# Two bias loads moved behind the DMA transposes, and a table of scheduler rules for 128 stretches of 16 score tiles

## The chip, the cores and the metric

The kernel runs on one core of a Trainium2 chip. The metric is device time in microseconds (us) of one execution; lower is better. Five engines are named as in the profile: PE (matrix), DVE (vector), ACT (activation functions), POOL and SP. SP issues every DMA of this kernel, all on one queue and in the order in which the program was built.

## The reference, cut to what matters

```python
xn = layernorm(x)                                  # x: 2048 x 640
qkv = (xn @ wqkv).reshape(S, 3, 32 heads, 20)      # attention with 32 heads of width 20
p = softmax(q @ k.T * 20 ** -0.5)                  # per head 2048 x 2048
s = (p @ v) @ wo                                   # per head, then 640 x 640
h = layernorm(xn)                                  # token MLP: it mixes the 2048 rows
u = gelu(h.T @ w1 + b1)                            # 640 x 1536
g = silu((u @ w2 + b2).T)                          # 2048 x 640
out = x + s * g
```

b1 (1536 values) and b2 (2048 values) are the two biases of the token MLP.

## The kernel before, in words

**Tiling.** The attention is cut into 8 head groups of 4 heads and 4 query blocks of 512, hence 32 passes; one pass has 16 key chunks of 128, each with 4 heads: 64 score tiles of 128 x 512, and 2048 tiles in all. Each tile is made by one matmul of 32 rows (`emit_st`, L1160), and up to four tiles of different heads can share the PE. A tile goes one of two ways. The ACT way: two or three tiles lie in neighbouring PSUM banks (`ACT_GROUPS`, L255: banks 0 to 2, and 3 and 4) and one ACT instruction takes the exponential of all of them into `pt_sb` (`emit_exp`, L1189). The DVE way: a whole key chunk (4 tiles, one per head) is turned into an approximate exponential by integer arithmetic on bfloat16 bit patterns: one DVE instruction per tile (L1200) and three shifted copies per chunk (L1224) that are averaged through pre-scaled copies of v (`vs_sb`). Chunks 2, 5, 8, 11 and 14 of a pass may go to the DVE (`RC`, L259). The products with v gather in bank 6 (L1240). At the end of a pass the DVE transposes and normalises the sum (`ep_steps`, L1334 to L1355).

**Stages.** First x and the weights are loaded. The layer norm of the 16 row blocks runs on DVE, with the power on POOL (`ln_steps`, L478 to L496). Blocks 0 to 3 are transposed on PE; blocks 4 to 15 by 12 DMA transposes (`xTd_steps`, L533), each of which waits for the L496 instruction of its block. Then the q and k projections of head group 0 (L573) and the v projections (L681). The other projections, the token MLP (L588, with evictions on L758 and the activation chain on L773 to L789) and the output projection (L872) are placed between the score tiles of later passes. The q and k of the other head groups travel through DRAM (L614, L653). Two small DMAs bring b1 and b2 into `bload_sb` (L444, L446; 2 bytes per element and partition), and two DVE instructions halve them (L1385, L1387).

**What sets the order.** Nothing is ordered on the chip. A planner in Python (`schedule`, from L403) keeps a model time for every engine and picks, in a loop (L1806), the next step of the engine that can start first; `pe_cands` (L1560) and `eng_cands` (L1781) list the candidates with a priority each. What it picks is appended to that engine's list, and every engine then executes its list strictly in order, with a semaphore wait wherever another engine's result is needed. Class constants steer the picks: `SLACK` and `MINJ` (how near to ACT's next need PE may start other work), `ROOM` (free slots of `pt_sb`), `LEND` (an ACT bank lent to a DVE tile), `LATE`, `PARTS`, `CONFL`, `FGAP` and others. The function `behind` (L1076) compares the projection and MLP work done with a straight line over the score tiles; when it is more than 3000 behind, the DVE may claim no new chunk (L1082) and may not use bank 7. DMAs are modelled by one bytes-per-time cost (`dma`, L166 and L412).

The lines that set a DMA's place and the DVE's share:

```python
def d_claimable():                                   # L1081
    if behind() > self.BEH_D:
        return None
...
add_job("bias", [ ...b1h on bl1..., ...b2h on bl2... ], ("xn15",), 43.0)   # L1384
```

Of the kernel before, what the change touches and what calls it, by code (L numbers as in the profile page):

```python
# [6 lines left out]
dt = mybir.dt  # L7
# [32 lines left out]
class Prog:  # L40
# [40 lines left out]
    def _add(self, eng, ceng, fn, reads, writes, name, extra_req=(), cost=100.0, tail=None):  # L81
# [51 lines left out]
        if ceng not in self.COMPUTE:  # L133
            start = max(start, 700.0)
            self.T[eng] = start + 450.0
            self.pipe = max(self.pipe, start + 600.0) + cost
            t.fin = self.pipe + (1200.0 if self.pipe < 2500.0 else 2800.0 if cost > 800.0 else 1400.0)
        else:
            self.T[eng] = start + cost
            self.busy[eng] += cost  # L140
            t.fin = start + cost + (self.TAIL[eng] if tail is None else tail)
# [23 lines left out]

    def dma(self, fn, reads=(), writes=(), name="dma", lane=None, cost=3000.0, over=()):  # L166
        if lane is None:
            lane = self.lane_rr
            self.lane_rr = (self.lane_rr + 1) % self.n_lanes
        ceng = f"d{lane}"  # L170
        prev = self.ctasks[ceng][-1] if self.ctasks[ceng] else None
        extra = [prev] if prev is not None else []
        for s in over:
            if s.w is not None:
                extra.append(s.w)
            extra.extend(s.readers.values())
        t = self._add("sp", ceng, fn, reads, writes, name, extra_req=extra, cost=cost)
        t.need_inc = True
        return t
# [67 lines left out]
class _Kern:  # L247
# [34 lines left out]
    QC = ((0.5, 3.0), (3.2, 6.4), (9.0, 13.5), (14.0, 18.0), (19.0, 22.0))  # L282
    LINE = (2.0, 31.7)
    BEH_D, BEH_J = 3000.0, 3000.0
    PARTS = (2,)
    DX = (1, 2, 3)
    XDC = 300000
    V1A, V1B = 0.8, 4.0
# [15 lines left out]
    def build(self):  # L304
# [4 lines left out]
        with es:  # L309
# [45 lines left out]
            pr.emit(sems)  # L355

    def schedule(self):
        pr, t, nc = self.prog, self.t, self.nc
# [53 lines left out]
        def dma(fn, reads, writes, name, nbytes, over=()):  # L412
            pr.dma(fn, reads=reads, writes=writes, name=name, cost=nbytes / 355.0, over=over)

# [24 lines left out]
        def small(fn):  # L439
# [3 lines left out]
            return f  # L443
        dma(small(lambda e: e.dma_start(bload_sb[:, 0:FC], B_b1.rearrange("(fc p) -> p fc", p=P))), [], [S_("bl1")],  # L444
            "dma_b1", 3000)
        dma(small(lambda e: e.dma_start(bload_sb[:, FC:FC + NB], B_b2.rearrange("(b p) -> p b", p=P))), [],  # L446
            [S_("bl2")], "dma_b2", 4000)

        pr.dve(lambda e: e.memset(on_sb[:], 0.0), writes=[S_("on")], name="on0", cost=200)
# [80 lines left out]
        def xTd_steps(b):  # L530
            dst = xnT_sb[:, :, b * 128:(b + 1) * 128]
            src = regC[:, b, :]
            return [("dma", lambda e: e.dma_start_transpose(dst, src), [S_(f"h{b}")], [S_(f"xTb{b}")], f"xTd{b}", self.XDC),  # L533
                    ("tag", f"xTd{b}")]
# [305 lines left out]
        def reload_steps():  # L840
            steps = []
            for c in range(4):
                for tb in range(NTB):
                    ws = S_(f"oTa_{c}_{tb}")
                    oT_slots.setdefault(("oTa", c), []).append(ws)
                    d = oT_sb[:, c, tb * 512:(tb + 1) * 512]
                    src = ok_dram[tb * 512:(tb + 1) * 512, c * 128:c * 128 + 128]
                    steps.append(("dma", lambda e, d=d, src=src: e.dma_start_transpose(d, src),
                                  [S_(f"okd{pass_of[(G, tb)]}_{g}") for G in range(L6) for g in range(GH)] + [S_("okz")], [ws],
                                  f"oTt{c}_{tb}", 131072, xall))  # L850
            return steps + [("tag", "oT")]
# [214 lines left out]
        def a_left(q):  # L1066
            n = sum(4 for c in range(NB) if (q, c) not in claimed)
            if a_cur[1] is not None and a_cur[0] == q:
                n += GH - a_cur[2]
            return n  # L1070

        jw = [0.0]
        JTOT = (self.NB * 5 * mm(480) + 36 * 5 * mm(512) + FC * NB * (mm(512) + mm(128)) * 2.0
                + 12 * 5 * (mm(512) + mm(128)))

        def behind():  # L1076
            x0, x1 = self.LINE
            x = nclaim[0] / UP
            return JTOT * min((x - x0) / (x1 - x0), 1.0) - jw[0]

        def d_claimable():  # L1081
            if behind() > self.BEH_D:  # L1082
                return None
# [29 lines left out]
        def d_bank():  # L1113
            if not dveready[0]:
                return None
            if dbank[0] == "free" and fin_bank(DB):
                return DB
            if self.SHARE and JB in freebanks and len(dop1) < 2 and not ramp[0] and behind() < self.BEH_J:
                return JB
# [256 lines left out]
        for g in range(GH):  # L1376
# [5 lines left out]
        add_job("qk1pad", pads, tuple(f"qk0_{w}_{tb}" for w in (0, 1) for tb in range(NTB)) + ("qk0_1_0a",), 41.0)  # L1382
        add_job("r2", r2_steps(), sum((xtag(gb) for gb in range(4)), ()), 43.0)
        add_job("bias", [  # L1384
            ("dve", lambda e: e.tensor_scalar(b1h_sb[:, :], bload_sb[:, 0:FC], 0.5, None, ALU.mult), [S_("bl1")],  # L1385
             [S_("b1h")], "b1h", 120.0),
            ("dve", lambda e: e.tensor_scalar(b2h_sb[:, :], bload_sb[:, FC:FC + NB], 0.5, None, ALU.mult), [S_("bl2")],  # L1387
             [S_("b2h")], "b2h", 120.0), ("tag", "bias")], ("xn15",), 43.0)

# [170 lines left out]
        def pe_cands(T):  # L1560
# [3 lines left out]
            if us:  # L1564
# [3 lines left out]
                for gi in range(len(self.ACT_GROUPS)):  # L1568
                    grp = self.ACT_GROUPS[(last_grp[0] + 1 + gi) % len(self.ACT_GROUPS)]
                    if grp_state[grp] == "free" and all(fin_bank(b) and b not in lent for b in grp):  # L1570
# [189 lines left out]
        def do_step(j, eng):  # L1760
            s = j.steps[j.i]
            j.i += 1
            if s[0] == "ev":
                n = s[8]
                fn = ev_fn(s, eng)
                cost = ac(n) if eng == "act" else (dv(n, 0.53) if s[7].startswith("xTe") else dp(n))
                getattr(pr, eng)(fn, reads=s[5], writes=s[6], name=s[7], cost=cost)
            elif s[0] == "pe":
                if j.bank and not ramp[0]:
                    jw[0] += s[5]  # L1770
                if len(s) > 6:
# [5 lines left out]
            else:  # L1777
                getattr(pr, s[0])(s[1], reads=s[2], writes=s[3], name=s[4], cost=s[5])
            settle(j)

        def eng_cands(eng, T):  # L1781
            c = []
            for j in active:
# [3 lines left out]
                elif s[0] == "ev" and (eng == "dve" or (eng == "act" and (ramp[0]))):  # L1787
                    c.append((min(j.prio - 3.0, 24.0) if not ramp[0] else j.prio - 3.0, pr.ready(eng, s[5], s[6]),
                              lambda j=j: do_step(j, eng)))
# [3 lines left out]
            if eng == "dve":  # L1793
# [3 lines left out]
                if dtop and tfree:  # L1797
                    d, k = dtop[0]
                    b0, b = d["tl"][0], tfree[0]
                    c.append((38.0, pr.ready("dve", [S_(f"dt{b0}_{g}") for g in range(4)],  # L1800
                                             [S_(f"dt{b}_{g}") for g in range(4)]), emit_top))
            return c

        bank_off = set()
        guard = 0
        while True:  # L1806
            guard += 1
            assert guard < 400000
            if ramp[0] and "v0_14" in done and "qk0_0_3" in done:
# [77 lines left out]
```

## Time and profile before

Seven runs: median 773.91 us (769.78 to 774.86). The profiled execution took 773.91 us itself, and its span from the first to the last instruction is 772.1 us, so 1.8 us lie around the span. Engine instructions before and after the change, as far as they differ, stand in the section on the change.

| | busy us | share of the span | instructions |
|---|---|---|---|
| PE matmuls | 729.9 | 95% | 10114 |
| DVE | 716.1 | 93% | 1348 |
| ACT | 737.3 | 96% | 709 |
| POOL | 13.2 | 2% | 19 |

How to read it: the busy time of an engine is the union of its records. Records of neighbouring ACT or DVE instructions overlap a little[...], so the mean length of a record times the count is more than the busy time. The chain of work that ended last runs through ACT for 75% of the span and through PE for 20%. The mean granted PE clock is 0.992 of full speed.

### The profile page before, as it was taken

How to read it: one execution, taken by the hardware profiler on the slowest of the kernel's cores; microseconds unless marked ns; L12 is line 12 of the kernel's file. 1: busy time of each engine (PE TensorE's matmuls, PEld its weight loads, DVE VectorE, ACT ScalarE, POOL GpSimd, SP SyncE). 2: the span in 40 equal slices, each digit the busy share in tenths (PEclk: the TensorE clock that was granted, in tenths of full speed). 3: DMA queues.
4: the chain of work that ended last, by engine and by line, in shares of the span. 5: the costliest groups of instructions: out<-in, count | busy, mean ns of one | idle time of the engine just before them, and what ended most of it. 6: DMA issues, size and time to landing. Idle time of an engine off the chain costs nothing.

```text
span 772.1 us, 22825 instructions
## 1 busy us (share of the span) xinstructions
PE 729.9 (95%) x10114; PEld 240.3 (31%) x10128; DVE 716.1 (93%) x1348; ACT 737.3 (96%) x709; POOL 13.2 (2%) x19
## 2 busy tenths in 40 slices
PE   8699999999999999999999999999999999999997
PEld 3232222223332322232322323232333332332222
DVE  7589999999999999898999999999999999999996
ACT  4599999999999999999999999999999999999993
POOL 3200000000000000000000000000000000000000
PEclk9899999999999999999999999999999999999999
DMA  9481111101120121031030014120335420041101
GB/s 265 85 161 43 34 30 33 23 18 27 38 64 13 20 51 45 16 84 20 14 84 12 19 27 93 45 53 6 96 78 69 122 65 18 7 149 46 48 12 69
DMA packets 117143, 42.53 MB, mean 55 GB/s; under 512 B 75300, under 2 KB 115876, under 8 KB 116996
## 3 DMA queue, kind: packets, MB, share of 16 engines
q1 hardware_dynamic: 117044, 41.07, 22.7%
q8 instruction: 79, 1.29, 0.7%
q14 instruction: 20, 0.16, 0.1%
HBM read 26.37 MB, written 10.22 MB: 47 GB/s over the span
## 4 chain that ended last, share of the span: by engine, by line
ACT 75%; PE 20%; DVE 2%; DMA 1%; issue 0%; SPq 0%; POOL 0%; ACTq 0%
ACT pt_sb L1189 73%; PE ps_all L1160 6%; PE ps_all L588 6%; PE ps_all L1240 5%; PE ps_all L872 1%; PE ps_all L573 1%; ACT zt_sb L779 1%; ACT zt_sb L784 1%; DMA wqk_sb<-in_A_wqkv_dram 1%; DMA xnT_sb<-regC 0%; SPq L418 0%; DVE dt_sb L1200 0%; PE ps_all L681 0%; DVE regC L496 0%; DVE dt_sb L1224 0%
## 5 line engine op out<-in xcount | busy, mean ns | idle before, releaser
L1189 ACT ACTIVATE pt_sb<-ps_all 128x1024 bf16<-128x1024 f32 (+1 forms) x671 | 717.1, 1203 | 3.6 <-PE ps_all L1160 2.5
L1200 DVE TENSOR_SCALAR dt_sb<-ps_all 128x512 uint16<-128x512 f32 x488 | 325.4, 680 | 25.9 <-PE ps_all L1160 24.7
L1160 PE MATMUL ps_all<-qk_sb 32*128 32x512 bf16 x2048 | 292.3, 386 | 27.1 <-ACT pt_sb L1189 23.6
L1224 DVE TENSOR_SCALAR dt_sb<-dt_sb 128x2048 uint16<-128x2048 uint16 x366 | 241.1, 684 | 1.7
L1160 PEld LDWEIGHTS ps_all<-qk_sb 32*128 32x128 bf16 x2048 | 74.2, 91 | 289.2 <-ACT pt_sb L1189 203.0
L1240 PE MATMUL ps_all<-pt_sb,v_sb 128*21 128x512 bf16 x1560 | 123.1, 382 | 0.1
L1240 PE MATMUL ps_all<-dt_sb,vs_sb 128*21 128x512 bf16 x1464 | 121.9, 384 | 0.0
L588 PE MATMUL ps_all<-regC,regA 128*32 128x512 bf16 (+1 forms) x1536 | 67.0, 301 | 0.0
L588 PE MATMUL ps_all<-regB,regA 128*32 128x128 bf16 (+1 forms) x1536 | 66.5, 301 | 0.1
L588 PE MATMUL ps_all<-xnT_sb,wqk_sb 128*32 128x512 bf16 x640 | 49.3, 383 | 0.3
L1240 PE MATMUL ps_all<-dt_sb,v_sb 128*21 128x512 bf16 x488 | 48.6, 389 | 0.6 <-DVE tr_sb L1334 0.5
L1240 PEld LDWEIGHTS ps_all<-pt_sb,v_sb 128*21 128x21 bf16 x1560 | 29.7, 91 | 51.1 <-issue 37.4
L1240 PEld LDWEIGHTS ps_all<-dt_sb,vs_sb 128*21 128x21 bf16 x1464 | 28.6, 91 | 32.3 <-issue 23.5
L588 PEld LDWEIGHTS ps_all<-regC,regA 128*32 128x32 bf16 x1536 | 28.8, 96 | 27.3 <-issue 13.1
L588 PEld LDWEIGHTS ps_all<-regB,regA 128*32 128x32 bf16 x1536 | 28.0, 96 | 26.5 <-issue 12.9
L872 PE MATMUL ps_all<-wv_sb,xnT_sb 128*128 128x128 bf16 (+3 forms) x150 | 27.3, 297 | 1.5 <-issue 1.3
L1334 DVE STREAM_TRANSPOSE tr_sb<-ps_all 128x512 f32<-128x512 f32 x32 | 22.6, 707 | 4.3 <-PE ps_all L1240 4.3
L588 PE MATMUL ps_all<-wv_sb,xnT_sb 128*32 128x480 bf16 x320 | 21.3, 369 | 0.0
L588 PEld LDWEIGHTS ps_all<-xnT_sb,wqk_sb 128*32 128x32 bf16 x640 | 14.0, 95 | 20.8 <-issue 10.0
L1240 PEld LDWEIGHTS ps_all<-dt_sb,v_sb 128*21 128x21 bf16 x488 | 12.2, 90 | 26.2 <-issue 21.2
L758 DVE TENSOR_SCALAR zt_sb<-ps_all,b2h_sb 128x512 bf16<-128x512 f32 (+1 forms) x32 | 17.1, 543 | 1.9 <-PE ps_all L588 1.8
L987 DVE CAST v_sb<-ps_all 128x480 bf16<-128x480 f32 (+1 forms) x23 | 13.8, 601 | 4.4 <-PE ps_all L681 3.6
(73 smaller groups left out, 293.3 us busy)
## 6 DMA issues: line engine op xcount, KB each, us to landing
regA<-in_B_w_dram SPq DMA_DIRECT2D x6, 1024.0 KB
regA<-in_B_w_dram SPq DMA_DIRECT2D x8, 768.0 KB
qk_sb<-qk_scratch_dram SPq DMA_DIRECT2D x56, 80.0 KB
qk_scratch_dram<-qs_sb SPq DMA_DIRECT2D x32, 128.0 KB
regA<-in_A_x_dram SPq DMA_DIRECT2D x6, 640.0 KB
ok_scratch_dram<-on_sb SPq DMA_DIRECT2D x96, 20.0 KB
out_dram<-regC SPq DMA_DIRECT2D x3, 640.0 KB
wqk_sb<-in_A_wqkv_dram SPq DMA_DIRECT2D x2, 480.0 KB
```

The source lines that it names most:

```text
L573: steps.append(("pe", lambda e, dc=dc, lhsT=lhsT: e.matmul(ps(bk, n), lhsT, xnT_sb[:, dc, tb * 512 + c0:tb * 512 + c0 + n], start=(dc == 0 ...
L588: fns.append(lambda e, c=c, e_=e_: e.matmul(oc(c, e_), lhsT[:, c:e_], rhs, start=start, stop=stop, tile_position=(0, c)))
L758: steps.append(("dve", lambda e, z=z, i=i, jj=jj: e.tensor_scalar(z[:, c0:c0 + n], ps(bk, n, i * n), 0.5, bias[:, jj:jj + 1], ALU.mult, AL ...
L779: steps.append(("act", lambda e: e.activation(tt_, tt_, AF.Tanh, scale=1.5957691216), [stt], [stt], f"th{j}", ac(640)))
L872: steps.append(("pe", lambda e, c=c, k=k: e.matmul(ap, oT_sb[0:k, c, b * 128:(b + 1) * 128], wo_ap[0:k, c, c0:c0 + n], start=(c == 0), sto ...
L987: return lambda e: e.tensor_copy(dst, src)
L1160: pr.pe(lambda e, outp=outp, lhsT=lhsT, rhs=rhs, g=g: e.matmul(outp, lhsT, rhs, start=True, stop=True, tile_position=(32 * g, 0)), reads=[ ...
L1189: tk = pr.act(lambda e: e.activation(outp, inp, AF.Exp, scale=math.log(2.0) / 128.0), reads=[bank_slot[b] for b in banks[:n]], writes=[S_( ...
L1200: tk = pr.dve(lambda e: e.tensor_scalar(w, src, WOFF, 0.0, ALU.add, ALU.max), reads=[bank_slot[bk]], writes=[S_(f"dt{d['tl'][0]}_{g}")], n ...
L1224: tk = pr.dve(lambda e: e.tensor_scalar(dst, src, dk, None, ALU.add), reads=[S_(f"dt{b0}_{g}") for g in range(4)], writes=[S_(f"dt{b}_{g}" ...
L1240: pr.pe(lambda e: e.matmul(outp, lhsT, rhs, start=(k == 0), stop=last, tile_position=(0, 32 * g)), reads=reads, writes=[bank_slot[AB]], na ...
L1334: steps.append(("dve", lambda e: e.transpose(tr_sb[:, :], ps(AB)), [bank_slot[AB]], [S_("tr")], f"epT{q}", 632.0))
```

## The change

1. The DMAs of b1 and b2 are no longer issued with the input loads. They become a job that starts after the four small copies inside `qk_sb` ("qk1pad"), so behind the 12 DMA transposes on SP's queue. The two DVE instructions that halve the biases move with them.
2. The planner gets a cost of its own for a DMA transpose: 1320 ns on the queue, and 2700 ns until it has landed.
3. `behind` is removed. What steered the DVE's claims and bank 7 by it is gone; in its place stands a flag `DON`.
4. Fourteen rules become settable (`OPTS`). A table `PLAN` has one row of 14 digits per stretch of 16 score tiles; at the start of each stretch `tune` sets the rules from its row.

```diff
-        dma(small(lambda e: e.dma_start(bload_sb[:, 0:FC], B_b1...)), [], [S_("bl1")], "dma_b1", 3000)
-        dma(small(lambda e: e.dma_start(bload_sb[:, FC:FC + NB], B_b2...)), [], [S_("bl2")], "dma_b2", 4000)
...
+        add_job("bload", [("dma", ...dma_b1...), ("dma", ...dma_b2...), ("tag", "bload")], ("qk1pad",), 43.0)
         add_job("bias", [ ...b1h..., ...b2h..., ("tag", "bias")],
-                ("xn15",), 43.0)
+                ("bload",), 43.0)
...
         def d_claimable():
-            if behind() > self.BEH_D:
+            if not self.DON:
                 return None
...
-            if self.SHARE and JB in freebanks and len(dop1) < 2 and not ramp[0] and behind() < self.BEH_J:
+            if self.SHARE and JB in freebanks and len(dop1) < 2 and not ramp[0]:
                 return JB
...
+    OPTS = (
+        ("SLACK", (120.0, 40.0, 200.0, 320.0)), ("MINJ", (640.0, 320.0, 1000.0)), ("ROOM", (3, 6, 0)),
+        ("DRIDE", (400.0, 150.0, 700.0)), ("LEND", (900.0, 300.0, 1500.0, 0.0, 2500.0)),
+        ("PARTS", ((2,), (2, 1), (3, 1), (1,), ())), ("LATE", (2.0, -9.0, 99.0)), ("DON", (True, False)),
+        ("LONE", (False, True)), ("CONFL", (True, False)), ("TOPP", (38.0, 22.0)), ("EVP", (24.0, 36.0)),
+        ("FGAP", (40.0, 150.0)), ("GROT", (1, 0)),
+    )
+    PLAN = ("00010000000000", "00000000000000", "00100000001000", ...)
+    def tune(self, w):
+        if w < len(self.PLAN):
+            for (name, vals), i in zip(self.OPTS, self.PLAN[w]):
+                setattr(self, name, vals[int(i)])
...
         while True:
             guard += 1
+            if nclaim[0] >= win * self.WIN:
+                self.tune(win)
+                win += 1
```

`LEND`'s first value is 900 where the constant was 1100. The functions that the steps call are the same as before; what the change makes of them is another order. What differs in the number of instructions, counted in the two built programs:

| instruction | before | after |
|---|---|---|
| exponential of 2 tiles, ACT (128 x 1024) | 453 | 423 |
| exponential of 3 tiles, ACT (128 x 1536) | 218 | 235 |
| exponential of 1 tile, ACT (128 x 512) | 0 | 1 |
| first DVE step of a tile (128 x 512) | 488 | 496 |
| shifted copy, DVE (128 x 2048) | 366 | 372 |
| matmul with zeros that keeps the PE active (L1255) | 116 | 104 |

All other instructions are the same in number, but for one q eviction in the ramp that the DVE does as a copy of k instead (and ACT the other). In the DVE's list the two halving instructions stood right behind the last layer norm block; now they stand behind the first six L1200 and three L1224 instructions. The order on PE, DVE, ACT and SP differs throughout.

## The prediction, made before the changed kernel was run

> **What bounds the kernel now.** I read the engines' busy row and the chain of waits first, then the costliest groups.
>
> ```profile
> span 772.1 us, 22825 instructions
> PE 729.9 (95%) x10114; PEld 240.3 (31%) x10128; DVE 716.1 (93%) x1348; ACT 737.3 (96%) x709; POOL 13.2 (2%) x19
> ...
> ACT 75%; PE 20%; DVE 2%; DMA 1%; issue 0%; SPq 0%; POOL 0%; ACTq 0%
> ...
> L1200 DVE TENSOR_SCALAR dt_sb<-ps_all 128x512 uint16<-128x512 f32 x488 | 325.4, 680 | 25.9 <-PE ps_all L1160 24.7
> ```
>
> ACT carries the chain. Three engines are over 90% busy, so the next question is where ACT is not. The groups by form and ACT's timeline tell it:
>
> ```profile
> L1189 ACT ACTIVATE pt_sb<-ps_all 128x1024 bf16<-128x1024 f32 x453 | 451.1, 1064 | 1.4 <-PE ps_all L1160 0.7 <-PE ps_all L1240 0.3
> L1189 ACT ACTIVATE pt_sb<-ps_all 128x1536 bf16<-128x1536 f32 x218 | 325.4, 1493 | 2.1 <-PE ps_all L1160 1.7 <-PE ps_all L1240 0.2
> ```
>
> ```profile
> 19.06 2.40 ACT L1189 ACTIVATE pt_sb<-ps_all 128x1024 bf16<-128x1024 f32 x2
> 28.45 0.60 ACT L986 ACTIVATE qk_sb<-ps_all 128x512 bf16<-128x512 f32 x1 [7.00 <-PE ps_all L573]
> 30.59 0.60 ACT L989 ACTIVATE qk_sb<-ps_all 128x512 bf16<-128x512 f32 x1 [1.54 <-PE ps_all L573]
> 31.13 1.02 ACT L1189 ACTIVATE pt_sb<-ps_all 128x1024 bf16<-128x1024 f32 x1
> ```
>
> Between 50 and 750 us ACT is busy 696.8 of 700 us (table of windows). Its one large hole is in the ramp: no exponential runs from 21.46 to 31.13. The chain there leads to a DMA transpose. SP's timeline and PE's:
>
> ```profile
> 8.64 2.67 SPq L423 DMA_DIRECT2D wqk_sb<-in_A_wqkv_dram  x2
> 11.36 2.15 SPq L444 DMA_DIRECT2D bload_sb<-in_B_b_dram  x1
> 13.55 4.17 SPq L446 DMA_DIRECT2D bload_sb<-in_B_b_dram  x1
> 17.76 22.36 SPq L533 DMA_TRANSPOSE xnT_sb<-regC  x12
> ```
>
> ```profile
> 20.44 1.04 PE L1255 MATMUL ps_all<-wp_sb,zw_sb 128*21 128x512 bf16 x16
> 26.50 4.05 PE L573 MATMUL ps_all<-xnT_sb,wp_sb 128*128 128x512 bf16 x9 [5.02 <-DMA xnT_sb<-regC]
> 30.48 1.03 PE L1160 MATMUL ps_all<-qk_sb 32*128 32x512 bf16 x5
> ```
>
> The two bias loads hold SP for 6.3 us right ahead of the transposes, while the first two blocks for these were normalised by 14.32 (L496 on DVE, 13.53 for 0.79 us). PE idles from 21.48 to 26.50, and then the clock is half:
>
> ```profile
> core 0: us, PE busy (x) PEld busy (x) DVE busy (x) ACT busy (x) POOL busy (x), PEclk, DMA share, GB/s
> 14.00:16.00 2.00, 2.00 (x23) 1.07 (x20) 1.16 (x5) 1.89 (x3) 0.69 (x1) 1.00 1.08 342
> 16.00:18.00 2.00, 1.80 (x17) 0.68 (x15) 1.97 (x9) 2.00 (x3) 0.00 (x0) 1.00 1.14 260
> 24.00:26.00 2.00, 0.00 (x0) 0.00 (x0) 2.00 (x6) 0.00 (x0) 0.00 (x0) 0.81 0.50 99
> 26.00:28.00 2.00, 1.50 (x4) 0.74 (x6) 1.32 (x7) 0.00 (x0) 0.00 (x0) 0.50 0.76 152
> ```
>
> **Step 1, the ramp.** Blocks 6 and 7 are normalised at 16.77 and 17.52, so by the L496 rows alone the fourth transpose could be issued at 17.5 to 18.1 and land 2.6 us later (the chain shows 2.59 from the issue at 23.46 to its landing), at 20.7. A rule speaks against so much: the Trainium skill, page "DMA: Bandwidth & Descriptors", section "Queues, rings and completion order", says that a DMA engine takes the descriptors of a queue in ring order. The transposes would then wait for the input loads ahead of them, and these move over 340 GB/s until 16 and end at about 17.2. Four transposes at the 1.23 us that one takes in the trace give 22.1, and with the completion up to 23.4. I take 22.0 for PE's start, nearer the rule, against 26.05 (23.46 + 2.59).
>
> PE then waits from about 21.5 to 22.0, not 5 us. The page "TensorE: Matmul & The Clock Gate", section "Part 1: The HAM clock gate", says that an idle window of about 3.4 us halves the clock; the trace agrees (0.81, then 0.50, after an idle stretch of 5.0 us). With at most 1.9 us idle (23.4 - 21.5) the clock stays, and the ten L573 matmuls take 10 x 0.22 = 2.2 us (five of them, warm, go by from 44.75 to 45.93) where 26.05 to 30.48 was 4.4. So: projections done 24.2, q eviction on ACT 0.6, first exponential 24.8 instead of 31.13: 6.3 us. Part is given back at the next blocks: the DVE evicts k ahead of normalising blocks 8 to 11, and PE may be late for their projection by 0 to 1.5 us; I take 0.7. **Net -5.6 us, between -3.5 and -7.**
>
> **Step 2, ACT's own work.** The tiles by ACT go from 453x2 + 218x3 = 1560 to 423x2 + 235x3 + 1 = 1552, in 659 instructions instead of 671. By the rows a third tile costs 1493 - 1064 = 0.429 us. The rest of an instruction is 1.064 - 0.858 = 0.206, of which 0.135 overlaps its neighbour ((453 x 1.064 + 218 x 1.493 - 717.1)/671), so 0.071. 8 x 0.429 + 12 x 0.071 = **-4.3 us**, all on ACT and so on the path.
>
> **Step 3, the DVE and PE.** Eight more tiles cost the DVE 8 x 0.667 (325.4/488) + 6 x 0.659 (241.1/366) = +9.3 us. They lie beside ACT: in the windows from 50 to 750 the DVE is busy 667.4 of 700, and L1200 waits for PE 24.7 us. If that cover were gone they would cost all 9.3. PE gets less to do: counted in the two orders there are 1206 instead of 1229 changes between score, product and full matmuls, about 0.10 each (a group of three scores starts at 14.14 and the next kind at 14.46; the wave itself takes 0.22), and 31 fewer score waves: 2.3 + 6.8 = 9 us. PE waits for ACT anyway, so I count nothing. The 12 fewer zero matmuls fill idle time: nothing.
>
> **Step 4, steady stalls.** L1189 takes 717.1/1560 = 0.460 us per tile over the whole run. Where ACT alone carries the chain (48.85 to 130.54, about 49 of two tiles and 27 of three) it is 81.69/179 = 0.456. So some 6 us of stalls are hidden in overlapping records and 3.3 us show after 33 us. A new order can win at most these 9 us and can lose about as much; no row tells which. PE's smaller load speaks for a gain, the DVE's larger one against. I take **-3.0 us**.
>
> **Step 5, the bias loads at their new place.** Nothing is won by them beyond step 1. On SP the first w1 load, q/k stores (first at 54.5) and okst stores now stand behind them: up to 6.3 us later. Nobody is near: the first MLP matmul comes after 331 of 2048 tiles, and the first reload after a store came 14 us ahead of any further need (74.6, for tiles that start after 256). The DVE is nearer. It halves b2 behind six L1200 and three L1224; queued behind that are the next L1200 and the transpose that ends pass 0, for which PE's products of pass 1 wait. The pad copies (48.88, 3.87 us) shift with the ramp to about 43.3, the loads then hold SP to 53.5 by their old durations and b2 lands near 55; the DVE arrives there at 43.8 (its first L1200 at 49.41, less 5.6) + 7.6 us of work = 51.4. A stall of the DVE of 0 (the 4.17 us were measured amid the input loads) to 4 us; I take 2, of which ACT sees 1 because two banks' groups are ahead of it. **+1.0 us, between 0 and 3.**
>
> **Step 6, the end.** From ACT's last exponential to the end are 12 us, alike in both orders; the last one has one tile instead of two: **-0.4**.
>
> **Sum.** 772.1 - 5.6 - 4.3 - 3.0 + 1.0 - 0.4 = 759.8 span; with the 1.8 around it 761.6. The profiled execution took 773.91, which is also the median of the seven, so this compares with the median directly.
>
> **Rivals.**
> A (likeliest, 0.60): as summed, 755 to 768.
> B (0.18): the new order also takes out nearly all steady stalls, the bias stall doesn't show: 772.1 - 6.3 - 4.3 - 9 - 0.4 + 1.8 = 753.9. For it: PE is 9 us lighter. Against: a fixed order meets durations that vary a little.
> C (0.13), slower: the DVE becomes the bound. Its place is the steady part. If its waits for PE (24.7 us at L1200) are not spare but come with the in-order lists, the 14 added instructions lengthen the run, and ACT waits instead: 772.1 - 5.6 + 9.3 + 1.0 + 1.8 = 778.6. It decides once the DVE's idle time doesn't shrink: then steps 2 and 4 vanish. For it: 93% busy, with idle before L1200 in 57 places. Against: ACT at 99.5% in the same windows, so it is ACT that the DVE's feeder serves.
> D (0.09): the ramp is won, but steady stalls grow by about 8 us, or the transposes are held back by the loads: 770 to 775, no change.
> About 0.3% (2.3 us) is what a measurement of this kernel can tell from no change. Faster A and B, 0.78; same D, 0.09; slower C, 0.13. The range 752 to 771 holds A, B and the edge of D.
>
> **What would show it.** SP: first L533-like issue near 14, none of the bias loads ahead of it. PE: no idle over 2 us between 21 and 26, PEclk 1.00 in all windows from 20 to 34. ACT: first exponential after the hole near 25 (step 1); exponentials' busy near 713 or less with idle after 33 us no more than 3 (steps 2 and 4). The DVE's wait for PE near 15 instead of 24.7 (step 3; if it stays near 25 and ACT's idle grows, C holds). A DVE wait for `bload_sb` at 50 to 56 (step 5). I am wrong if the transposes land after 25 anyway, if ACT idles over 10 us after 33 us, or if a DMA that PE waits for appears in the middle of the run.

## The result and the profile after

| kernel | runs | median us | ratio to before, 95% |
|---|---|---|---|
| before | 36 | 772.62 (769.78 to 774.86) | 1 |
| changed | 15 | 770.36 (767.23 to 771.74) | 0.9964 [0.9953, 0.9974] |

Faster, by 0.36% or 2.8 us, where 1.6% was forecast. The profiled execution of the changed kernel took 768.43 us, 1.9 under its median; that of before lay 1.3 above its own (772.62 in 36 runs, 773.91 in the seven known earlier). The two profiles differ by 5.5 us, twice what the runs do, so times are compared by the ratios below and the profiles only show where.

The page after, and ACT's groups by form:

```profile
span 766.6 us, 22854 instructions
PE 730.4 (95%) x10125; PEld 243.1 (32%) x10140; DVE 721.8 (94%) x1362; ACT 733.6 (96%) x697; POOL 13.7 (2%) x19
...
ACT 67%; PE 24%; DVE 4%; DMA 3%; SPq 1%; issue 1%; DVEq 0%; ACTq 0%
...
L1240 DVE TENSOR_SCALAR dt_sb<-ps_all 128x512 uint16<-128x512 f32 x496 | 331.8, 681 | 21.8 <-PE ps_all L1200 20.3
```

```profile
L1229 ACT ACTIVATE pt_sb<-ps_all 128x1024 bf16<-128x1024 f32 x423 | 425.7, 1065 | 3.3 <-PE ps_all L1200 2.6
L1229 ACT ACTIVATE pt_sb<-ps_all 128x1536 bf16<-128x1536 f32 x235 | 350.4, 1491 | 2.8 <-PE ps_all L1200 2.4
```

Lines have moved: the exponential is L1229 (it was L1189), the score matmul L1200 (L1160), the DVE's first step L1240 (L1200), the product with v L1280, the transposes L581. ACT's share of the chain fell from 75% to 67%; DMA rose from 1% to 3%. The exponentials' waits for scores grew, 2.6 and 2.4 us instead of 0.7 and 1.7.

The ramp, on SP, PE and ACT:

```profile
8.90 2.46 SPq L476 DMA_DIRECT2D wqk_sb<-in_A_wqkv_dram  x2
14.21 24.68 SPq L581 DMA_TRANSPOSE xnT_sb<-regC  x12
...
47.93 0.88 SPq L1425 DMA_DIRECT2D bload_sb<-in_B_b_dram  x1
48.85 1.37 SPq L1427 DMA_DIRECT2D bload_sb<-in_B_b_dram  x1
```

```profile
20.66 0.60 PE L1295 MATMUL ps_all<-wp_sb,zw_sb 128*21 128x512 bf16 x8
23.84 2.10 PE L621 MATMUL ps_all<-xnT_sb,wp_sb 128*128 128x512 bf16 x9 [2.58 <-DMA xnT_sb<-regC]
```

```profile
25.98 0.60 ACT L1037 ACTIVATE qk_sb<-ps_all 128x512 bf16<-128x512 f32 x1 [4.31 <-PE ps_all L621]
26.48 1.02 ACT L1229 ACTIVATE pt_sb<-ps_all 128x1024 bf16<-128x1024 f32 x1
...
35.75 1.45 ACT L1229 ACTIVATE pt_sb<-ps_all 128x1536 bf16<-128x1536 f32 x1 [1.15 <-PE ps_all L1200]
```

The first transpose is issued at 14.21 instead of 17.76, and ACT resumes at 26.48 instead of 31.13: the lead is real, 4.65 us. Then I counted tiles along ACT's exponentials, before against after: tile 17 is done at 32.0 / 27.4 us, tile 32 at 39.7 / 34.4, tile 64 at 55.4 / 52.6, tile 80 at 62.7 / 62.5. By tile 80 of some 1550 the whole lead is gone. (Each such time is where ACT stands after so many tiles; what it loses is that time less its exponentials' own work, an estimate from their distances in the records: 0.427 us a tile and 0.05 an instruction.) Some 2.5 us of the lead go between tiles 32 and 64. The remaining 2.6 us go in one place, between 54 and 62 us:

```profile
54.38 0.17 DVE L1430 TENSOR_SCALAR b1h_sb<-bload_sb 128x12 f32<-128x12 bf16 x1 [1.25 <-DMA bload_sb<-in_B_b_dram]
55.22 0.17 DVE L1432 TENSOR_SCALAR b2h_sb<-bload_sb 128x16 f32<-128x16 bf16 x1 [0.67 <-DMA bload_sb<-in_B_b_dram]
```

```profile
54.25 0.39 PE L1200 MATMUL ps_all<-qk_sb 32*128 32x512 bf16 x2
56.05 0.40 PE L1200 MATMUL ps_all<-qk_sb 32*128 32x512 bf16 x4 [1.41 <-DVE dt_sb L1240]
```

```profile
core 0: us, PE busy (x) PEld busy (x) DVE busy (x) ACT busy (x) POOL busy (x), PEclk, DMA share, GB/s
54.00:56.00 2.00, 0.64 (x10) 0.09 (x2) 0.95 (x4) 1.92 (x2) 0.00 (x0) 1.00 1.16 274
56.00:58.00 2.00, 1.73 (x20) 0.61 (x24) 2.00 (x5) 1.45 (x1) 0.00 (x0) 0.65 1.20 291
58.00:60.00 2.00, 2.00 (x23) 0.44 (x19) 0.89 (x2) 0.01 (x1) 0.00 (x0) 0.50 1.19 290
```

```profile
56.52 1.45 ACT L1229 ACTIVATE pt_sb<-ps_all 128x1536 bf16<-128x1536 f32 x1 [0.60 <-PE ps_all L1200]
59.99 3.50 ACT L1229 ACTIVATE pt_sb<-ps_all 128x1024 bf16<-128x1024 f32 x3 [2.02 <-PE ps_all L1200]
```

Read in this order: the DVE stands before the halving for 1.25 and 0.67 us, because the biases have not landed. PE, which needs a bank (a part of PSUM, the memory that PE writes its results to) that the DVE must empty, is idle for 1.41 us. Then its clock is 0.50 until 60, so it is busy and slow, and from 58 to 60 ACT gets nothing (0.01 us busy). The last wait of the chain names PE, but what set it off is a DMA of 4 KB.

### The profile page after: what moved, and what is told of

It is laid out like the page before. It is cut to its first block, busy times and chain, and to the rows that moved or that the text cites. A ratio compares the mean times of both kernels' runs of the same rounds, so it can differ in the third digit from the quotient of the medians.

```text
span 766.6 us, 22854 instructions
## 1 busy us (share of the span) xinstructions
PE 730.4 (95%) x10125; PEld 243.1 (32%) x10140; DVE 721.8 (94%) x1362; ACT 733.6 (96%) x697; POOL 13.7 (2%) x19
## 4 chain that ended last, share of the span: by engine, by line
ACT 67%; PE 24%; DVE 4%; DMA 3%; SPq 1%; issue 1%; DVEq 0%; ACTq 0%
ACT pt_sb L1229 65%; PE ps_all L1200 8%; PE ps_all L1280 7%; PE ps_all L636 6%; PE ps_all L920 2%; DVE dt_sb L1240 2%; PE ps_all L621 1%; DMA xnT_sb<-regC 1%; ACT zt_sb L827 1%; ACT zt_sb L832 1%; DVE dt_sb L1264 1%; DMA bload_sb<-in_B_b_dram 1%; DMA wqk_sb<-in_A_wqkv_dram 1%; DVE v_sb L1035 0%; SPq L1417 0%
## 5 line engine op out<-in xcount | busy, mean ns | idle before, releaser
L1229 ACT ACTIVATE pt_sb<-ps_all 128x1024 bf16<-128x1024 f32 (+1 forms) x659 | 713.1, 1216 | 6.1 <-PE ps_all L1200 5.1
L1240 DVE TENSOR_SCALAR dt_sb<-ps_all 128x512 uint16<-128x512 f32 x496 | 331.8, 681 | 21.8 <-PE ps_all L1200 20.3
L1200 PE MATMUL ps_all<-qk_sb 32*128 32x512 bf16 x2048 | 291.4, 386 | 21.1 <-ACT pt_sb L1229 16.7
L1264 DVE TENSOR_SCALAR dt_sb<-dt_sb 128x2048 uint16<-128x2048 uint16 x372 | 247.0, 684 | 1.5
L1200 PEld LDWEIGHTS ps_all<-qk_sb 32*128 32x128 bf16 x2048 | 76.0, 91 | 281.5 <-ACT pt_sb L1229 189.9
L1280 PE MATMUL ps_all<-dt_sb,vs_sb 128*21 128x512 bf16 x1488 | 127.3, 384 | 0.3 <-DVE dt_sb L1264 0.2
L1280 PE MATMUL ps_all<-pt_sb,v_sb 128*21 128x512 bf16 x1552 | 124.0, 384 | 0.0
L1280 PE MATMUL ps_all<-dt_sb,v_sb 128*21 128x512 bf16 x496 | 49.3, 388 | 1.7 <-DVE tr_sb L1374 1.6
L1280 PEld LDWEIGHTS ps_all<-dt_sb,vs_sb 128*21 128x21 bf16 x1488 | 32.3, 91 | 41.7 <-issue 22.1
L1280 PEld LDWEIGHTS ps_all<-pt_sb,v_sb 128*21 128x21 bf16 x1552 | 29.1, 91 | 47.8 <-issue 38.4
L636 PEld LDWEIGHTS ps_all<-regC,regA 128*32 128x32 bf16 x1536 | 28.6, 96 | 26.2 <-issue 12.3
L1280 PEld LDWEIGHTS ps_all<-dt_sb,v_sb 128*21 128x21 bf16 x496 | 12.4, 90 | 25.1 <-issue 17.1
```

The costliest lines, as they stand in the source:

```text
L636: fns.append(lambda e, c=c, e_=e_: e.matmul(oc(c, e_), lhsT[:, c:e_], rhs, start=start, stop=stop, tile_position=(0, c)))
L1200: pr.pe(lambda e, outp=outp, lhsT=lhsT, rhs=rhs, g=g: e.matmul(outp, lhsT, rhs, start=True, stop=True, tile_position=(32 * g, 0)), reads=[ ...
L1229: tk = pr.act(lambda e: e.activation(outp, inp, AF.Exp, scale=math.log(2.0) / 128.0), reads=[bank_slot[b] for b in banks[:n]], writes=[S_( ...
L1240: tk = pr.dve(lambda e: e.tensor_scalar(w, src, WOFF, 0.0, ALU.add, ALU.max), reads=[bank_slot[bk]], writes=[S_(f"dt{d['tl'][0]}_{g}")], n ...
L1264: tk = pr.dve(lambda e: e.tensor_scalar(dst, src, dk, None, ALU.add), reads=[S_(f"dt{b0}_{g}") for g in range(4)], writes=[S_(f"dt{b}_{g}" ...
L1280: pr.pe(lambda e: e.matmul(outp, lhsT, rhs, start=(k == 0), stop=last, tile_position=(0, 32 * g)), reads=reads, writes=[bank_slot[AB]], na ...
```

## The experiments

Theory: the ramp's lead is real and is spent again at the bias wait, and partly where the DVE evicts k ahead of normalising blocks 8 to 11. Rivals: the lead is absorbed downstream whatever happens to these waits; or the table costs what the ramp wins. Nearly all kernels below keep the planned order of a kernel and move single steps in it (`move(step, n, (other, m))` puts the n-th step of that name ahead of the other; the waits follow from the new order). Nothing of the computation is left out in any of them. Ratios are to the kernel before, each measured beside it.

| run | edit | median us | ratio, 95% |
|---|---|---|---|
| e1_bias_early | changed, biases ahead of the transposes | 769.43 | 0.9963 [0.9950, 0.9976] |
| e2_halve_late | changed, halving at the end of pass 1 | 766.03 | 0.9916 [0.9900, 0.9931] |
| e3_norm_first | changed, blocks 8 to 11 ahead of k | 769.29 | 0.9965 [0.9953, 0.9976] |
| e4_both | e2 and e3 | 765.53 | 0.9905 [0.9889, 0.9921] |
| e5_no_table | changed, empty table | 797.85 | 1.0322 [1.0301, 1.0342] |
| e6_before_moved | before, biases behind, halving late | 770.02 | 0.9963 [0.9949, 0.9978] |
| e7_fill_stall | changed, zeros in the stall | 768.54 | 0.9947 [0.9930, 0.9965] |
| e8_fill_ramp | e2, zeros in the ramp | 766.76 | 0.9921 [0.9904, 0.9937] |
| e9_w_late | e2, two weight loads later | 764.95 | 0.9888 [0.9866, 0.9909] |
| e10_before_w_late | e6, two weight loads later | 768.31 | 0.9931 [0.9913, 0.9949] |
| e11_bias_mid | changed, biases right behind the transposes | 766.57 | 0.9909 [0.9888, 0.9930] |

**e1: undo the move of the loads.**

```diff
+for name in ("dma_b1", "dma_b2"): move(name, 0, ("xTd4", 0))
```

> The changed kernel's order, but the two bias DMAs stand on SP right ahead of the first DMA transpose, as before the change; the halving stays where the change put it. Theory (the ramp's lead is real and is spent again, about half of it on the wait of the halving for the late bias DMAs): PE's first projection starts near 26 at half clock, the exponentials resume near 31 as before the change, the DVE's waits for bload_sb at 54.4 and 55.2 (1.25 and 0.67 us) are gone; tile 80 is reached within 1 us of the changed kernel's 62.5, and the time is the changed kernel's, 0 to +2 us. Rival 1 (the move of the DMAs is worth its whole lead at the end, and the table costs it elsewhere): +4 to +5 us against the changed kernel. Rival 2 (early bias DMAs are better, the wait costs more than the lead): -1 to -3 us.

0.9963, where the changed kernel has 0.9964: taking back the edit that the change is named for costs nothing. In its profile PE starts at 26.29 with half clock, ACT resumes 4 us later than in the changed kernel, no step waits for the biases, and tile 80 is done at 63.3 (62.5). So what the lead wins is what the wait costs. Rival 1 is out. Of the tiles from 17 to 50, e1 loses 3.2 us without any lead, the changed kernel 3.7 and the kernel before 1.5: what goes there belongs mostly to the new order and not to the ramp.

**e2: the halving 20 us later, the loads where the change put them.**

```diff
+for name in ("b1h", "b2h"): move(name, 0, ("epT1", 0))
```

> The changed kernel, but the two halving instructions on the DVE stand right ahead of the transpose that ends pass 1, some 20 us later; the bias DMAs stay behind the transposes. Theory: no DVE instruction waits for bload_sb, so L1240 at 56 and ACT's stalls of 0.60 and 2.02 us at 56 to 61 are gone; -2 to -3 us, about 767.5. Rival 1 (ACT stalls there anyway: PE or DVE are late for those tiles without the bias wait, or the lead is absorbed later): within 0.7 us of the changed kernel. Rival 2 (the halving at its new place delays the end of pass 1): +0.5 to +2.

0.9916 against 0.9964: 3.7 us (0.0048 of 772.6) come back by moving two instructions of 0.17 us. The intervals don't touch. From 50 to 64 us ACT is busy 13.9 of 14 us and the clock is 1.00. The 1.7 us that its profile leads the changed kernel's by at tile 80 (60.8 against 62.5) are still 1.6 at the last tile (752.8 against 754.4): the rival "absorbed downstream" falls.

**e3: blocks 8 to 11 ahead of the k eviction; e4: both.**

```diff
+for n in range(4):
+    move("ln8ap", n, ("qke0_1_1", 0)); move(f"xTd{8 + n}", 0, ("qke0_1_1", 0))
```

> The changed kernel, but the four normalising DVE instructions of row blocks 8 to 11 and their four DMA transposes stand ahead of the k eviction for which the DVE waited 3.48 us at 24.9 (their powers on POOL were ready near 22.3). Theory: these transposes are issued near 23 instead of 25.98, PE's projection of the third quarter comes about 2.5 us earlier, ACT's stall of 1.15 us at 35.8 shrinks; -1 to -2.4 us if the lead is kept, but some of it turns into a longer wait for the biases, so -0.5 to -2. Rival (the k eviction becomes the late step, or the rest absorbs it): 0 to +1.

> The changed kernel with both edits: normalising and transposes of blocks 8 to 11 ahead of the k eviction, and the halving of the biases at the end of pass 1. Theory: tile 80 is reached near 58 to 59 instead of 62.5 and the lead lasts; -4 to -5 us, about 766. Rival (the lead over the order before is absorbed by PE or DVE in the steady part, which were both over 93% busy): within 1 us of the changed kernel, with the lead at tile 80 shrinking to under 1 us by tile 1000.

e3 is the changed kernel's time (0.9965), but its profile had half clock in the ramp, so by itself it tells little. e4, whose profile kept the clock there, gains what e2 gains within the error (0.9905, 0.9916). The second half of my theory falls. The four transposes are issued at 23.17 in e4 instead of 25.98, but ACT's stall near 36 us is 1.14, as it was. In the changed kernel PE waits for no DMA there: it runs eight projections and eight products (from 32.95 to 35.31) in a row ahead of the next scores. That is the order, not a late transpose.

**e5: without the table.**

```diff
-    PLAN = ("00010000000000", ...)
+    PLAN = ()
```

> The changed kernel with an empty table: every rule stays at its first value, the planner builds its order anew; the bias loads stay behind the transposes. It tells what the table alone is worth. The prediction counted -7.3 us for what the table makes of the order (steps 2 and 4); the first four runs leave about -3 of the changed kernel's gain when the ramp is undone (0.9963 of the time before). Theory (the table is worth less than predicted): +2 to +4 us against the changed kernel, so the time before or a little above. Rival 1 (the table is worth what was predicted, something else took it away): +6 to +8. Rival 2 (the table is worth nothing, the gain of 3 us is the planner's own change): -1 to +1.

All three expectations were wrong: 1.0322 against 0.9964 is 28 us. The end of e5, on ACT and then on PE:

```profile
742.30 24.58 ACT L1206 ACTIVATE pt_sb<-ps_all 128x1024 bf16<-128x1024 f32 x23
```

```profile
767.64 3.58 PE L897 MATMUL ps_all<-wv_sb,xnT_sb 128*128 128x512 bf16 x24
...
773.54 4.48 PE L897 MATMUL ps_all<-wv_sb,xnT_sb 128*128 128x512 bf16 x24
...
791.10 0.56 PE L897 MATMUL ps_all<-wv_sb,xnT_sb 128*128 128x128 bf16 x5 [0.39 <-DVE regC L912]
```

The last exponential ends at 766.9 of 795.8 us, so 29 us of output projection stand behind it; in the changed kernel 12 us do. These 17 us are the larger part of the 28. The rest stands ahead of it: ACT's last exponential comes 12 us later than in the changed kernel, and by the count of tiles it loses that between tile 80 and the end (44.0 us against 32.1). The function `behind`, which the change removed, compared the work done with a straight line over the run; that the table now does this in its place fits the tail, but putting `behind` back was not tried. "The table" is therefore no extra on top of the order before; what the change as a whole makes of the order is told by the pairs e2/e6 and e9/e10.

**e6: the moved loads without the new order.**

```diff
+for name in ("dma_b2", "dma_b1"): move_after(name, 0, ("qkpad3", 0))
+for name in ("b1h", "b2h"): move(name, 0, ("epT1", 0))
```

> The kernel before in its own order, with one edit: the two bias DMAs stand behind the four copies inside qk_sb, and the halving right ahead of the transpose that ends pass 1. No table. Theory (the ramp's lead of 3.3 to 5 us, by whether PE's clock is halved after its wait for the transposes, is kept to the end where nobody waits for the biases): -3.5 to -5 us against the kernel before, ratio 0.9935 to 0.9955; PE starts its projections near 23.7. Rival (the order before has no use for the lead: a later wait, such as a DMA, takes it): ratio 0.998 to 1.001.

0.9963, -2.8 us, with nobody waiting for the biases: at the weak end. PE started at 23.82, and its first nine projections took 3.01 us. The clock fell in the middle of them.

**e7: keep the bias wait, keep PE busy in it.**

```diff
+i = at("st1_5_3"); rec[i:i] = zs * 5            # zs: four zero matmuls, one wave
+for g in range(4): move(f"pv0_14_{g}", 0, ("st1_5_3", 0))
```

> The changed kernel, wait for the biases kept, with 20 matmuls with zeros (5 waves of about 0.26 us) on PE where it idled from 54.6 to 56.05; the last four products of pass 0 stand behind them so that they add to an open sum. It parts the price of the DVE's wait (1.25 + 0.67 us) from that of PE's half clock after it (0.50 from 57 to 60). Theory (most of the 3.4 us that ACT loses there is the half clock): PE's clock stays at 1.00 from 55 to 61, ACT's stalls of 0.60 and 2.02 us shrink to about 0.5 together; -1.5 to -2.5 us. Rival (the DVE's wait itself is the price, the clock only goes along): 0 to -0.5. If the clock is halved with the zeros as well: 0 to +1.

The profile, windows and ACT:

```profile
56.00:58.00 2.00, 1.57 (x32) 0.62 (x28) 1.92 (x5) 1.59 (x2) 0.00 (x0) 1.00 1.19 290
58.00:60.00 2.00, 2.00 (x27) 0.51 (x19) 2.00 (x5) 1.23 (x3) 0.00 (x0) 1.00 1.20 291
```

```profile
56.58 1.45 ACT L1265 ACTIVATE pt_sb<-ps_all 128x1536 bf16<-128x1536 f32 x1 [0.41 <-PE ps_all L1236]
58.73 31.50 ACT L1265 ACTIVATE pt_sb<-ps_all 128x1024 bf16<-128x1024 f32 x29 [0.70 <-PE ps_all L1236]
```

The DVE waits as before (1.18 and 0.56 us), the clock stays at 1.00, and ACT's two stalls are 1.11 us instead of 2.62. In the count of tiles ACT loses 4.8 us from tile 32 to 80, the changed kernel 6.6, e2 3.2. So of the 3.4 us that the wait costs there, about 1.8 would be the half clock and 1.6 the wait. This rests on one profile of each kernel, and the edit also put four products later. The ratio (0.9947) points the same way, 1.3 us, but its interval overlaps the changed kernel's: that the half clock carries half of the price is not shown by the times.

**e8: keep PE busy in the ramp.**

```diff
+i = at("qk0_1_1"); rec[i:i] = zs * 9
```

> The kernel with the halving late (e2_halve_late) and 36 more matmuls with zeros (9 waves of about 0.26 us) on PE where it waited for the transposes, from 21.1 to 23.6. Its profile showed the ten projections at half clock, 4.02 us after a wait of 2.51, while the changed kernel's took 2.10 after a wait of 2.58. Theory (whether the clock falls there is a toss between executions, and activity decides it): with the zeros the clock is 1.00 from 22 to 28 and the ten projections take 2.1 to 2.3 us in each execution; -0.5 to -1.5 us in the median against e2_halve_late. Rival (the zeros end after the transposes have landed and delay PE): 0 to +0.5.

What it tests is seen by setting e2's profile beside that of the changed kernel above, whose order is the same up to there (PE, then windows with half clock):

```profile
23.63 4.02 PE L654 MATMUL ps_all<-xnT_sb,wp_sb 128*128 128x512 bf16 x10 [2.51 <-DMA xnT_sb<-regC]
```

```profile
24.00:26.00 2.00, 2.00 (x6) 0.69 (x5) 0.11 (x1) 0.00 (x0) 0.00 (x0) 0.50 0.00 0
```

A wait of 2.51 us was followed by half clock here, one of 2.58 by full clock there. Of eight profiles with a wait of 2.4 to 3.0 us (changed, e2 to e7, e11) the clock stayed in three and fell in five, at once or a little later. The Trainium skill, page "TensorE: Matmul & The Clock Gate", section "Part 1: The HAM clock gate", says that the gate judges a window of about 3.4 us that runs freely. The traces agree. In each profile the half-clock stretches (but for the one that the end of the run cuts short) last 3.41 or 6.83 us and begin whole multiples of 3.413 us apart; in the changed kernel they begin at 56.60 and 667.59. Where this grid lies differs between profiles. In the five profiles in which the clock fell, 2.36 to 2.66 us of the wait lie within one step of the grid; in the other three the grid cuts the wait, and no step holds more than 1.88. So the same wait costs the clock or not by where it falls on the grid. With the zeros the clock stayed in e8's profile (nine projections in 2.10 us), but the time is e2's (0.9921, 0.9916): the gain that was expected is not there. Its profile shows where it went:

```profile
34.66 1.89 PE L657 MATMUL ps_all<-xnT_sb,wp_sb 128*128 128x512 bf16 x8 [1.48 <-DMA xnT_sb<-regC]
```

PE came earlier to the next projection and waited there for blocks 8 to 11; of 1.3 us of lead over e2 at tile 17, 0.5 is left at tile 80. So the late transposes that e3 could not show are next in line once the first four are early.

**e9 and e10: two loads of 1 MB in all out of the transposes' way.**

```diff
+for name in ("dma_w256", "dma_w896"): move_after(name, 0, ("xTd15", 0))
```

> The kernel with the halving late (e2_halve_late) with one more edit: the two loads of the q and k weights of the other head groups (1 MB, first read at 48.7) stand behind the last DMA transpose instead of behind x. It tests why the fourth transpose, issued at 18.76, had landed only near 23.6, where the prediction had 22.0. Theory (the transposes wait for the input loads in front of them, which move 330 GB/s until 17.5): some 3 us of loads less, so PE starts its projections at 20.8 to 22 instead of 23.6, its idle time shrinks from 2.5 to under 1 us and its clock stays whole; first exponential after the hole near 25; -2 to -3.5 us against e2_halve_late, 762.5 to 764. Rival 1 (the transposes are slow by themselves: 4.8 us from issue to landing whatever is ahead): PE starts at 23.6 as before, within 0.7 us of e2_halve_late. Rival 2 (PE starts early, but blocks 8 to 11 come late as before and ACT waits there): -0.5 to -1.5.

> The kernel before in its own order with the biases moved and halved late (e6_before_moved), and in addition the same two weight loads behind the last DMA transpose. Theory: PE starts at 20.8 to 22, the whole of step 1 as predicted (-5.6 us) is there in an order without the table: ratio 0.992 to 0.994 against the kernel before, 2 us less than e6_before_moved. Rival (the transposes are slow by themselves): 0.9963 as e6_before_moved. Together with e9 it gives what the table is worth a second time: the prediction's steps 2, 4 and 6 say -7.7 us, the first comparison (e2 against e6) said -3.6.

e9 on PE and ACT:

```profile
22.25 2.33 PE L656 MATMUL ps_all<-xnT_sb,wp_sb 128*128 128x512 bf16 x10 [1.11 <-DMA xnT_sb<-regC]
```

```profile
24.62 0.60 ACT L1072 ACTIVATE qk_sb<-ps_all 128x512 bf16<-128x512 f32 x1 [3.07 <-PE ps_all L656]
```

The fourth transpose was issued at 19.56 and PE started 2.7 us later; in the changed kernel it was issued at 18.76 and PE started 5.1 us later. The page "DMA: Bandwidth & Descriptors", section "Queues, rings and completion order", has each DMA engine take descriptors in ring order: the transposes stood behind the loads, as that rule says and as I had weighed it, but for longer. (Loads and transposes also share the DMA engines; these runs don't part that from the order of the ring.) PE starts 1.4 us earlier than in e2, its idle time is 1.1 us, the clock stays, and ACT goes on 3 us earlier. e9 has 0.9888, e2 0.9916; e10 has 0.9931, e6 0.9963: 2.2 and 2.5 us, with intervals that overlap in each pair but the same sign and size in both. (The medians alone differ by 1.1 and 1.7 us; the kernel before, measured beside e9 and e10, was slower than beside e2 and e6, which the ratios take out.) e9 is the fastest kernel of the study, 1.1% under before.

**e11: the biases right behind the last transpose, the halving left.**

```diff
+for name in ("dma_b2", "dma_b1"): move_after(name, 0, ("xTd15", 0))
```

> The changed kernel, but the two bias DMAs stand right behind the last DMA transpose, ahead of the small stores and copies that are issued from 38.94 to 47.88; the halving stays where the change put it. Theory (the DVE's wait comes only from the place on SP; the DMAs take 4 to 6.5 us from issue to landing): they are issued near 39 to 42, land by 48, the halving at 53 to 54 waits for nothing, PE's clock stays whole from 55 to 61; -3 to -4 us, as with the halving late, 766 to 767. Rival (the bias DMAs delay the copies inside qk_sb, for which the scores of head group 0 wait, or the first MLP load): 0 to -1, with a new wait of PE for these.

```profile
54.30 0.17 DVE L1463 TENSOR_SCALAR b1h_sb<-bload_sb 128x12 f32<-128x12 bf16 x1
54.37 0.17 DVE L1465 TENSOR_SCALAR b2h_sb<-bload_sb 128x16 f32<-128x16 bf16 x1
```

Issued at 40.20 and 40.82 instead of 47.93 and 48.85, the biases were there when the halving came, at 54.3. 0.9909, 4.2 us under the changed kernel: the second mend of the same wait gives what the first gave, and the copies that now stand behind them cost nothing that shows.

## Why the prediction was wrong

The direction was right; the size was not, -2.8 us where 12 were counted. In the runs' own terms, with 772.6 for 1:

| term | predicted | measured | from |
|---|---|---|---|
| ramp (step 1) | -5.6 | -2.8 | e6 / before |
| new order (steps 2, 4, 6) | -7.7 | -3.6, -3.3, -2.8 | e2 / e6, e9 / e10, e1 / before |
| bias wait (step 5) | +1.0 | +3.7, +4.2 | changed / e2, changed / e11 |
| sum | -12.3 | -1.9 to -2.7 | measured whole: -2.8 |

Each ratio to before is uncertain by 0.8 to 1.6 us to either side, and a term that divides two of them by some 1.5 to 2. The three terms along one chain (e6 / before, e2 / e6, changed / e2) give the whole by construction, so that sum, -2.7, checks nothing. What they rest on is that other kernels give each of the last two terms again (e9 / e10 and e1 / before, changed / e11); with these the sum is -1.9, within the error of -2.8. Step 6 predicted -0.4 and is part of the second row.

**Step 1, the ramp: right mechanism, half the size.** The transposes were issued at 14.21 as said, and ACT resumed earlier. But PE started at 23.84, not 22.0. The term that failed is the landing: I took 22.0 "nearer the rule", which is where four transposes end by that rule (22.1) with nothing for the completion, although my own sum with it was 23.4. With the loads out of the way (e10) the ramp gives -5.3 us (ratio 0.9931), near the predicted -5.6. The second failed term is "the clock stays": it did so in three of eight profiles, at 2.1 to 2.3 us for the projections instead of 3.0 to 4.0. That PE idled for less than 3.4 us did not keep the clock: 2.36 us of a wait within one step of the grid were followed by its fall (e6). The 0.7 us given back at the next blocks was 2.2: from tile 17 to 50 ACT loses 3.7 us in the changed kernel and 1.5 before. e4, with the transposes earlier, still loses 3.3 there, and e1, with the ramp of before, 3.2, so it is mostly PE's and ACT's own order and not the wait that I named.

**Step 2, ACT's own work: right.** The exponentials are busy 713.1 us, against 717.1 before and 713 as given; between e10 and e9, alike in the ramp, it is 717.1 against 712.6: -4.5, predicted -4.3.

**Step 3, the DVE's added work is hidden: right.** Rival C didn't come. The DVE's wait for PE fell from 24.7 to 20.3, not to 15.

**Step 4, steady stalls -3.0: wrong, in sum they did not shrink.** Per tile the exponentials take 713.1/1552 = 0.459 us, before 0.460; where ACT alone carried the chain it was 0.456. From 50 to 750 us, e10 (order before) and e9 (new order):

```profile
50.00:750.00 700.00, 673.77 (x9692) 216.75 (x9692) 669.30 (x1207) 697.68 (x671) 0.63 (x1) 1.00 0.21 46
```

```profile
50.00:750.00 700.00, 679.57 (x9739) 220.87 (x9738) 675.24 (x1220) 698.53 (x662) 1.10 (x1) 1.00 0.21 48
```

ACT is busy 697.7 and 698.5 us of 700: 0.8 us apart. With step 2 confirmed at -4.3 to -4.5, the measured -2.8 to -3.6 for the order leaves steps 4 and 6 together at +0.7 to +1.7, uncertain by 1.5 to 2, instead of -3.4. That is a rest, not a measurement of its own. The count of tiles shows two parts of it, from one profile of each kernel. From tile 17 to 50 the order before loses 1.5, 2.0 and 2.7 us (before, e6, e10), the new order 3.1 to 4.0 in all its profiles (e5 left out). From tile 80 to the last exponential the order before loses 33.8, 34.2 and 32.8 us, the new order 31.2 to 32.3 in eight of nine; e4, with three half-clock stretches there, loses 35.5. So the new order seems to win some 1.5 us in the steady part and to lose about as much right behind the ramp. Which rows of the table do it was not tried.

**Step 5, the bias wait: the wait right, its price not.** Predicted: b2 lands near 55, the DVE stalls 2 us. Measured: it landed by 55.2, the DVE stalled 1.92. That these agree is in part luck: I had the loads hold SP until 53.5 and the DVE arrive at 51.4, where SP was free of them at 50.22, the landing took 5 us more, and the DVE arrived at 53.1. What failed is "of which ACT sees 1 because two banks' groups are ahead of it": it cost 3.7 us, above even the upper bound of 3. The groups ahead did not cover it, because PE was idle too, for 1.41 us, and then ran 3.4 us at half clock, in which it could not refill them. The price is shown by e2 and e11; how it parts into the wait (about 1.6 us) and the clock (1.8) is e7's, from one profile.

**Step 6** can't be told apart: from ACT's last exponential to the end are 12 us in both.

**The signs I had set.** First transpose near 14: yes. No PE idle over 2 us between 21 and 26: no, 2.58. Clock 1.00 from 20 to 34: in this profile yes, in e2's not. First exponential near 25: no, 26.48. Exponentials' busy time near 713: yes. DVE wait for the biases at 50 to 56: yes, and the view ahead of it should have been PE's clock.

Rival D had the time (770.4 lies in its 770 to 775) and half of the cause: the transposes were held back by the loads, for 1.8 us. Its other half did not come: what ate the lead stands ahead of tile 80, at the blocks behind the ramp and at 54 to 62 us, and steady stalls did not grow by 8.

## What to carry to other kernels

When a load is moved out of a queue's way, look for who waits for it at the new place, and price that wait on the engine that feeds the bound, with its clock: here a wait of 1.9 us on the DVE left PE idle for 1.4, and ACT lost 3.4 in the profiles. If the consumer can wait (here two instructions of 0.17 us whose result is needed far later), move it as well; that was worth more than the change. And when a transfer's start is brought forward, ask what is still in front of it on the same rings: moving two weight loads behind the transposes gave 2 us more.

## What the runs showed of the hardware

- A wait of PE of 2.4 to 3.0 us was followed by half clock in five profiles and by full clock in three. The clock falls only on a grid of 3.413 us whose place differs between profiles; it fell where 2.36 us or more of the wait lay in one step and stayed where at most 1.88 did. Idle time alone is not the measure: 1.41 us at 54.6 in the changed kernel, within the step that ended at 56.60, was followed by 3.4 us of half clock, and what else counts stays open. Still shorter waits stood ahead of a fall elsewhere: 0.48 and 0.53 us near 666 in the changed kernel lie ahead of a clock of 0.76 from 665 to 670, and the same two in e9's profile (near 662) are followed by full clock.
- The times of single executions go with the granted clock. Of the changed kernel's 16, four at 0.990 took 771.0 to 771.7 us, six at 0.993 took 770.2 to 770.8, five at 0.996 to 0.998 took 767.2 to 768.4. Over the 16 that is 0.5 us for each 0.001. Most of the spread of "equal" runs goes with it.
- The two bias loads, 7 KB together, held SP for 0.88 and 1.37 us but had landed only by 54.4 and 55.2, 5 us after their issue ended; from 51 to 52 the DMA engines moved 3 GB/s at a busy share of 2.00. SP had been held for 2.15 and 4.17 us by the same loads amid the input: the time SP is held says little about the landing.
